# The last load of Wo in two pieces, and the residual's copies of x in four

## The chip, the cores and the metric

The kernel runs on one core of one Trainium2 chip. The metric is device time in microseconds of one execution, the median over several. A core has five engines with an instruction queue each: TensorE (PE; its weight loads are listed as PEld), VectorE (DVE), ScalarE (ACT), GpSimd (POOL) and SyncE (SP), and sixteen DMA engines that work on what the queues issue. In the profile SPq, ACTq and POOLq are the queues as issuers.

## What is computed

One decode step of an attention block beside a gated MLP, on 8 rows (batch 8, one token) of 512 numbers in bf16:

```python
xn = layernorm(x)
q  = xn @ wq                                # 32 heads of 128
k, v = the last 2048 of 8192 positions of the caches, 8 heads, each used by 4 query heads
s  = softmax(q k^T / sqrt(128)) v @ wo
g  = silu((sigmoid(xn @ w_gate) * (xn @ w_up)) @ w_down)
return x + s * g
```

The caches' windows are 64 MB, the weights another 13 MB; all are read once.

## The kernel before

**Tiles and loads.** Keys and values come in 32 tiles of 2 MB (`k_sb`, `v_sb`: one batch row and four of the eight heads each). They share a ring of ten buffers with the two halves of Wq, the three MLP weights and the two halves of Wo. All of these loads are issued on SP's queue, line 86, in one order: Wq's halves; key and value tiles, each value tile some slots behind its keys; the three MLP weights before the last two value tiles; last Wo. `issue_loads` issues as many as there are free buffers. The halves of Wo are cut: the first in two loads of 1 MB, the second in three of 512 KB and two of 256 KB (`load_wo`). The groups (h0, h1, j0, j1) of that list are the head groups and, in them, which of four interleaved rows j of Wo are loaded.

**The order of the work.** After the layer norm (`x_f` to `xnT_sb`, lines 259 to 287) PE makes q from `xnT_sb` and Wq. Then 64 slots follow: PE transposes a quarter of a key tile (line 395), DVE copies the result, PE multiplies by q (line 411); softmax runs once per batch row, and PE multiplies probabilities and values eleven slots later (line 513). After the last key slot comes the MLP, then the rest of the value products. The tail: 64 matmuls with Wo into `a_ps` (line 624; for each of eight head groups and four j, two column halves on different rows of PE's array), DVE's product with `gate` (`prod`, line 634), DVE's sum with x (`y_bf`, line 636), and two output transfers, on SP and ScalarE (line 638).

**The copies of x.** `x_bf` (line 92, ScalarE's queue) feeds the layer norm. The last sum uses another copy, `x2_sb` (`x_sb` in the profile, where digits are left out): columns 0 to 255 of x stand on partitions 0 to 7, columns 256 to 511 on partitions 32 to 39. GpSimd clears it (line 175) and issues its two loads (line 177), ahead of building the constants `ident`, `SumM` and `ones`, which DVE's constants and the layer norm's transposes need.

**Queues and counters.** Each queue runs its instructions in order; an instruction that waits holds up all behind it. The program's waits are made when it is built. Each transfer has a completion counter: those issued by SP and ScalarE share eight (0 to 7), given out in turn in the order of the built program, and GpSimd's have eight others. A transfer waits until the one that had its counter before has landed; so SP's loads have at most eight under way. `x_bf` has counter 0, Wq's halves 1 and 2, and the first key tile 3. At the end (line 667) SP waits for all counters and engines in a list of seven steps and a drain: counter 1; 2 and 0; 3 and GpSimd's second; 4 and GpSimd's first; 5 and DVE; 6 and PE; 7 and ScalarE; then GpSimd. A barrier over all engines follows.

Of the kernel before, what the change touches and what calls it, by code (L numbers as in the profile page):

```python
# [10 lines left out]
def kernel(  # L11
# [13 lines left out]
    nc = tc.nc  # L25
    P = 128
    B, _, D = A_x.shape
# [29 lines left out]
    DC = D // NCOL  # L57
# [25 lines left out]
    def load(dst, src, q=None):  # L83
        if q is None:
            q = nc.sync
        q.dma_start(out=dst, in_=src)

    def ring_tile(shape, name):
        return ring.tile(shape, bf16, name=name, tag="ring", align_bytes=ALIGN)
# [57 lines left out]
    def load_wo(half):  # L147
        t = ring_tile([P, HG // 2, 4, D], f"wo_sb{half}")
        for h0, h1, j0, j1 in (
            ((0, 2, 0, 4), (2, 4, 0, 4)),  # L150
            ((4, 5, 0, 4), (5, 6, 0, 4), (6, 7, 0, 4), (7, 8, 0, 2), (7, 8, 2, 4)),
        )[half]:
            o = half * (HG // 2)
            load(t[:, h0 - o : h1 - o, j0:j1, :], wo_view[:, h0:h1, j0:j1, :])
            for hg in range(h0, h1):
                for j in range(j0, j1):
                    wo_parts[hg, j] = t[:, hg - o, j, :]

    def issue_loads():
        while loads_done[0] < len(loads) and free_bufs[0] > 0:  # L160
            kind, i = loads[loads_done[0]]
            if kind == 0:
                k_tiles[i] = load_kv(A_k_cache, i, "k_sb")
            elif kind == 1:
                v_tiles[i] = load_kv(A_v_cache, i, "v_sb")
            elif kind == 2:
                load_mlp(i)
            else:
                load_wo(i)
            loads_done[0] += 1  # L170
            free_bufs[0] -= 1

    issue_loads()
    x2_sb = work.tile([NCOL * 32, DC], bf16, name="x2_sb")
    nc.gpsimd.memset(x2_sb[:], 0.0)
    for j in range(NCOL):
        nc.gpsimd.dma_start(
            out=x2_sb[32 * j : 32 * j + B, :],
            in_=A_x.flatten_outer_dims()[:, DC * j : DC * (j + 1)],
        )  # L180


    ident = consts.tile([P, P], bf16, name="ident")
# [3 lines left out]
    for off in range(-rep * (NJ - 1), rep * NJ, rep):  # L187
        nc.gpsimd.affine_select(
            out=SumM[:],
            in_=SumM[:],  # L190
# [9 lines left out]
        out=SumM_blk,  # L200
        in_=SumM_blk,
# [7 lines left out]
        out=SumM_blk,  # L209
        in_=SumM_blk,  # L210
# [11 lines left out]
        out=Jneg[:],  # L222
        in_=ident[:].rearrange("p (a j r) -> p j a r", j=NJ, r=rep),
# [4 lines left out]
        out=Jneg[:], in0=Jneg[:], scalar1=-scale, scalar2=None, op0=ALU.mult  # L228
# [4 lines left out]
        out=Hm[:],  # L233
        in_=ident[:].rearrange("p (a gl) -> p gl a", gl=GL),
# [6 lines left out]
        out=Sel[:],  # L241
        in_=ident[:].rearrange("p (a m) -> p m a", m=32),
# [6 lines left out]
        out=perm[:].rearrange("k (p gl) -> k p gl", gl=GL),  # L249
        in_=ident[:].rearrange("k (gl p) -> k p gl", gl=GL),  # L250
# [17 lines left out]
        out=rstd[:], in_=mv[:, 1:2], func=AF.Sqrt, bias=eps_t[:], scale=1.0  # L268
# [4 lines left out]
        out=xn_bf[:],  # L273
# [7 lines left out]
    for kt in range(KT):  # L281
        nc.tensor.transpose(  # L282
            out=xnT_ps[:, kt, :], in_=xn_bf[:B, kt::KT], identity=ident[:B, :B]
# [353 lines left out]
    for c in range(NCOL):  # L637
        queues[c].dma_start(
            out=out.flatten_outer_dims()[:, DC * c : DC * (c + 1)],
            in_=y_bf[32 * c : 32 * c + B, :],  # L640
# [31 lines left out]
```

## Time and profile before

| what | value |
|---|---|
| median of 3 runs | 199.86 us (199.71 to 199.94) |
| the profiled execution: its own time | 199.68 us |
| its span, first to last instruction | 197.9 us |
| PE busy, share of the span | 156.5 us, 79% |
| DVE busy | 121.7 us, 62% |
| ACT busy, POOL busy | 22.9 us, 7.4 us |
| moved by DMA | 81.33 MB, 6724 packets, mean 411 GB/s |
| loads of key tiles, issue to landing (median) | 38.9 us |
| loads of 256 KB of Wo: two, issue to landing (median) | 16.9 us |
| copies of x for the last sum: two of 4 KB, issue to landing (median) | 6.1 us |

Times in the profile are microseconds from the first instruction; durations of single instructions are in nanoseconds. A wait is put down to what ended it. The duration of a DMA instruction is that of its issue; a transfer is done at its landing. A median over an even number of transfers is the mean of the middle two: the two of 256 KB took 14.80 and 19.07 us.

### The profile page before, as it was taken

How to read it: one execution, taken by the hardware profiler on the slowest of the kernel's cores; microseconds unless marked ns; L12 is line 12 of the kernel's file. 1: busy time of each engine (PE TensorE's matmuls, PEld its weight loads, DVE VectorE, ACT ScalarE, POOL GpSimd, SP SyncE). 2: the span in 40 equal slices, each digit the busy share in tenths (PEclk: the TensorE clock that was granted, in tenths of full speed). 3: DMA queues.
4: the chain of work that ended last, by engine and by line, in shares of the span. 5: the costliest groups of instructions: out<-in, count | busy, mean ns of one | idle time of the engine just before them, and what ended most of it. 6: DMA issues, size and time to landing. Idle time of an engine off the chain costs nothing.

```text
span 197.9 us, 4704 instructions
## 1 busy us (share of the span) xinstructions
PE 156.5 (79%) x2088; PEld 102.2 (52%) x2088; DVE 121.7 (62%) x256; ACT 22.9 (12%) x48; POOL 7.4 (4%) x20
## 2 busy tenths in 40 slices
PE   0164999689979898968996979697999896757692
PEld 0113766456646555635564656464755573244581
DVE  2607788687787587748774677278758775231211
ACT  2001000500110021002100110012002102400000
POOL 7700000000000000000000000000000000000000
PEclk9999999999999999999998899979999999675558
DMA  6999999999999999999999999999999999999980
GB/s 227 429 427 440 437 421 427 421 439 424 431 427 427 427 434 427 431 427 431 427 431 432 421 434 427 437 421 431 427 424 440 426 424 432 428 425 420 416 331 31
DMA packets 6724, 81.33 MB, mean 411 GB/s; under 512 B 776, under 2 KB 816, under 8 KB 1968
## 3 DMA queue, kind: packets, MB, share of 16 engines
q1 hardware_dynamic: 6608, 81.01, 96.4%
q8 instruction: 16, 0.26, 0.5%
q10 hardware_dynamic: 32, 0.01, 0.1%
q14 instruction: 4, 0.03, 0.0%
q0 software_dynamic: 64, 0.01, 0.0%
HBM read 81.02 MB, written 0.01 MB: 409 GB/s over the span
## 4 chain that ended last, share of the span: by engine, by line
DMA 89%; PE 7%; DVE 2%; issue 0%; SPq 0%
DMA k_sb<-in_A_k_cache_dram 60%; DMA v_sb<-in_A_v_cache_dram 18%; DMA wo_sb<-in_A_wo_dram 7%; DMA wq_sb<-in_A_wq_dram 4%; PE kT_ps L395 4%; PE s_ps L411 1%; DVE kT_sb L398 1%; PE acc_ps L513 1%; DVE pT_sb L473 1%; DVE pt_bf L451 0%; DVE prod L634 0%; DVE y_bf L636 0%; PE a_ps L624 0%; PE pT_ps L457 0%; PE den_ps L495 0%
## 5 line engine op out<-in xcount | busy, mean ns | idle before, releaser
L398 DVE COPY kT_sb<-kT_ps 128x1024 bf16<-128x1024 bf16 x128 | 83.5, 687 | 35.6 <-PE kT_ps L395 35.0
L395 PE MATMUL kT_ps<-ident,k_sb 128*128 128x128 bf16 x1024 | 72.0, 226 | 9.7 <-DMA k_sb<-in_A_k_cache_dram 9.5
L395 PEld LDWEIGHTS <-k_sb 128*128 128x128 bf16 x1024 | 62.2, 102 | 30.9 <-issue 16.7
L411 PE MATMUL s_ps<-kT_sb,qz_sb 128*32 128x512 bf16 x256 | 39.9, 612 | 0.0
L513 PE MATMUL acc_ps<-v_sb,pT_sb 128*32 128x256 bf16 x512 | 27.3, 300 | 4.1 <-DVE pT_sb L473 2.6
L513 PEld LDWEIGHTS <-pT_sb 128*32 128x32 bf16 x512 | 13.0, 105 | 16.6 <-issue 12.0
L534 PEld LDWEIGHTS oT_ps<-Sel,acc_sb 128*128 128x128 f32 x64 | 9.6, 215 | 9.2 <-issue 5.8
L526 ACT COPY acc_sb<-acc_ps 128x256 f32<-128x256 f32 x16 | 5.9, 372 | 70.0 <-PE acc_ps L513 70.0
L534 PE MATMUL oT_ps<-Sel,acc_sb 128*128 128x16 f32 x64 | 11.1, 289 | 2.0 <-ACT acc_sb L526 1.1
L437 ACT ACTIVATE p_bf<-s_ps,nm 128x512 bf16<-128x512 f32 x8 | 5.5, 687 | 49.2 <-DVE nm L434 49.2
L411 PEld LDWEIGHTS <-qz_sb 128*32 128x32 bf16 x256 | 6.6, 93 | 6.9 <-issue 0.8
L457 PE MATMUL pT_ps<-pt_bf,perm 128*128 128x512 bf16 x8 | 3.1, 385 | 7.7 <-DVE pt_bf L451 7.7
L473 DVE TENSOR_SCALAR pT_sb<-pc_bf,Hm 128x512 bf16<-128x512 bf16 x32 | 9.0, 345 | 0.0
L282 PE MATMUL xnT_ps<-ident,xn_bf 8*128 8x8 bf16 x4 | 0.3, 174 | 8.7 <-DVE xn_bf L272 8.7
L451 DVE STREAM_TRANSPOSE pt_bf<-p_bf 128x512 bf16<-128x512 bf16 x8 | 5.6, 704 | 1.7 <-ACT p_bf L437 1.7
L541 DVE TENSOR_TENSOR oT_sb<-oT_ps,rden 128x16 bf16<-128x16 f32 x16 | 2.7, 171 | 6.0 <-PE oT_ps L534 6.0
L624 PE MATMUL a_ps<-wo_sb,o_sb 128*32 128x256 bf16 x64 | 6.2, 369 | 0.2 <-DMA wo_sb<-in_A_wo_dram 0.2
L423 DVE TENSOR_REDUCE mx<-s_ps 128x1 f32<-128x512 f32 x8 | 5.5, 682 | 0.6 <-PE s_ps L411 0.6
L348 PE MATMUL q_ps<-wq_sb,xnT_sb 128*32 128x512 bf16 x32 | 3.8, 627 | 2.2 <-DMA wq_sb<-in_A_wq_dram 2.0
L624 PEld LDWEIGHTS <-o_sb 128*32 128x32 bf16 x64 | 4.9, 131 | 1.2 <-issue 0.4
L465 ACT CAST pc_bf<-pT_ps 128x512 bf16<-128x512 f32 x8 | 4.7, 586 | 6.6 <-PE pT_ps L457 6.6
L497 DVE RECIPROCAL rden<-den_ps 128x32 f32<-128x32 f32 x8 | 2.9, 358 | 4.2 <-PE den_ps L495 4.2
(61 smaller groups left out, 56.1 us busy)
## 6 DMA issues: line engine op xcount, KB each, us to landing
k_sb<-in_A_k_cache_dram SPq DMA_DIRECT2D x16, 2048.0 KB, 38.9
v_sb<-in_A_v_cache_dram SPq DMA_DIRECT2D x16, 2048.0 KB, 39.3
wq_sb<-in_A_wq_dram SPq DMA_DIRECT2D x2, 2048.0 KB, 9.7
wo_sb<-in_A_wo_dram SPq DMA_DIRECT2D x2, 1024.0 KB, 32.3
wg_sb<-in_B_w_gate_dram SPq DMA_DIRECT2D x1, 1792.0 KB, 38.2
wu_sb<-in_B_w_up_dram SPq DMA_DIRECT2D x1, 1792.0 KB, 35.3
wd_sb<-in_B_w_down_dram SPq DMA_DIRECT2D x1, 1792.0 KB, 37.0
wo_sb<-in_A_wo_dram SPq DMA_DIRECT2D x3, 512.0 KB, 24.1
```

The source lines that it names most:

```text
L395: nc.tensor.transpose(out=kT_ps[:, jj, :], in_=k_sb[:, c0 + jj, :], identity=ident[:, :])
L398: nc.vector.tensor_copy(out=kT_tiles[t][:, h2 * HALF : (h2 + 1) * HALF, :], in_=kT_ps[:])
L411: nc.tensor.matmul(s_tiles[b][XR * gl : XR * (gl + 1), :], lhsT=qz_sb[:, b, GL * gg + gl, z0 : z0 + XR], rhs=kT[:, :, gl::GL], start=(x == 0),
L423: nc.vector.reduce_max(out=mx[:], in_=s_tiles[b][:], axis=AX.X)
L437: nc.scalar.activation(out=p_bf[:], in_=s_tiles.pop(b)[:], func=AF.Exp, bias=nm[:], scale=scale, accum_out=den128[:],)
L451: nc.vector.transpose(out=pt_bf[:], in_=p_bf[:])
L465: nc.scalar.copy(out=pc_bf[:], in_=pT_ps[:])
L473: nc.vector.tensor_scalar(out=pT_tiles[b][:, :, gl, :], in0=pc, scalar1=Hm[:, gl : gl + 1], scalar2=None, op0=ALU.mult,)
L513: nc.tensor.matmul(acc_tiles[i][32 * c : 32 * (c + 1), :], lhsT=pT_tiles[b][:, x * (CC // 2) + n, :, :].rearrange("p g n -> p (g n)"), rhs ...
L526: nc.scalar.copy(out=acc_sb[:], in_=acc_tiles.pop(i)[:])
L534: nc.tensor.matmul(oT_ps[:], lhsT=acc_sb[:, Dh * c2 : Dh * (c2 + 1)], rhs=Sel[:].rearrange("p (g c r) -> p c g r", g=GL, c=2)[:, c2], star ...
L624: nc.tensor.matmul(a_ps[32 * c : 32 * (c + 1), :], lhsT=o2_sb[:, hg, j, :], rhs=wo_parts[hg, j][:, DC * c : DC * (c + 1)], start=(n == 0), ...
```

## The change

The last 256 KB of Wo (head group 7, j = 2 and 3) are loaded as two transfers of 128 KB, one for each j, so that a partition's row of the transfer has 1 KB in place of 2. The two loads of `x2_sb` become four, each of four rows and 256 columns; the first column half is issued by GpSimd in two, the second by ScalarE in two. In the code they stand where the two stood: after the first round of loads and after GpSimd's clearing, ahead of the constants; on ScalarE that is behind `x_bf` and ahead of the layer norm's square root (line 267).

```diff
@@ load_wo
         for h0, h1, j0, j1 in (
             ((0, 2, 0, 4), (2, 4, 0, 4)),
-            ((4, 5, 0, 4), (5, 6, 0, 4), (6, 7, 0, 4), (7, 8, 0, 2), (7, 8, 2, 4)),
+            ((4, 5, 0, 4), (5, 6, 0, 4), (6, 7, 0, 4), (7, 8, 0, 2), (7, 8, 2, 3), (7, 8, 3, 4)),
         )[half]:
@@ after the first issue_loads()
     x2_sb = work.tile([NCOL * 32, DC], bf16, name="x2_sb")
     nc.gpsimd.memset(x2_sb[:], 0.0)
+    BH = B // 2
     for j in range(NCOL):
-        nc.gpsimd.dma_start(
-            out=x2_sb[32 * j : 32 * j + B, :],
-            in_=A_x.flatten_outer_dims()[:, DC * j : DC * (j + 1)],
-        )
+        for h in range(2):
+            (nc.gpsimd, nc.scalar)[j].dma_start(
+                out=x2_sb[32 * j + BH * h : 32 * j + BH * (h + 1), :],
+                in_=A_x.flatten_outer_dims()[
+                    BH * h : BH * (h + 1), DC * j : DC * (j + 1)
+                ],
+            )
```

## The prediction

> **What bounds the kernel now.** I read the page first, for the share of the transfers and the chain that ended last.
>
> ```profile
> span 197.9 us, 4704 instructions
> ...
> DMA  6999999999999999999999999999999999999980
> ...
> DMA 89%; PE 7%; DVE 2%; issue 0%; SPq 0%
> ```
>
> The reader is to see that the sixteen DMA engines are full from the second of forty slices to the last but two: 81 MB at 411 GB/s is the kernel. The change alters no bytes of any size, so what it can move lies before the stream starts or after its end. The chain of waits in order of time shows the end (start, duration, what):
>
> ```profile
> 179.27 14.80 DMA wo_sb<-in_A_wo_dram
> 194.07 0.04 issue
> 194.11 0.41 PE a_ps L624 x4
> 194.52 0.02 issue
> 194.55 0.42 DVE prod L634
> 194.97 0.02 issue
> 195.00 0.42 DVE y_bf L636
> ```
>
> The last piece of Wo is issued at 179.27, lands at 194.07, and only the four matmuls that read it (j = 2 and 3, two column halves each), the product and the sum follow. The windows of the tail (engine columns, then granted clock, DMA share, GB/s) say whether PE could use an earlier piece:
>
> ```profile
> 190.00:191.00 1.00, 1.00 (x14) 0.85 (x10) 0.00 (x0) 0.00 (x0) 0.00 (x0) 0.50 0.97 379
> 191.00:192.00 1.00, 1.00 (x14) 0.83 (x12) 0.00 (x0) 0.00 (x0) 0.00 (x0) 0.50 0.59 225
> 192.00:193.00 1.00, 1.00 (x16) 0.90 (x14) 0.00 (x0) 0.00 (x0) 0.00 (x0) 0.66 0.55 217
> 193.00:194.00 1.00, 0.92 (x16) 0.59 (x11) 0.00 (x0) 0.00 (x0) 0.00 (x0) 1.00 0.33 125
> ```
>
> PE is busy to 193.92, at half clock until about 192.7, and starves only for the last 0.19 us. The DMA share of 0.55 to 0.59 says that about half of the engines were done by 191 and the other half run on to 193.8.
>
> Then the start, from the timeline of all engines (the first number in brackets is idle time before, then its cause):
>
> ```profile
> 0.80 0.60 ACTq L92 DMA_DIRECT2D x_bf<-in_A_x_dram  x1
> 1.41 1.17 POOL L177 DMA_DIRECT2D x_sb<-in_A_x_dram  x2 [0.30 <-POOL x_sb L175]
> 1.44 1.28 ACT L267 ACT_TABLE_LOAD   x1 [1.44 <-PEq L656]
> 7.57 0.29 ACT L267 ACTIVATE rstd<-mv,eps_t 8x1 f32<-8x1 f32 x1 [4.85 <-DVE eps_t L265]
> 13.10 1.90 PE L348 MATMUL q_ps<-wq_sb,xnT_sb 128*32 128x512 bf16 x16 [1.97 <-DMA wq_sb<-in_A_wq_dram]
> ```
>
> ScalarE's queue is free from 2.72 (end of the table load) to 7.57, and PE waits 1.97 us for the second half of Wq, which is cover for anything that delays the layer norm. Last, SP's waits at the end (total, times, longest) and its semaphore instructions of the closing line:
>
> ```profile
> SPq L638 <- DMA wo_sb<-in_A_wo_dram: 5.1, 1, 5.1
> ...
> SPq L667 <- DMA out_dram<-y_bf: 0.2, 1, 0.2
> ```
>
> ```profile
> L667 SPq EVENT_SEMAPHORE  x9: 17/28/28, 195.9 to 197.8; - x9
> ```
>
> The first row is the rule of the eight completion counters: SP's output transfer may not start before the transfer that used its counter last has landed, here the first piece of Wo at 186.6. The 0.2 is in the closing list of waits: four of its seven steps had run before the outputs were in, and it stopped at the counters of the two output transfers (landed at 196.73 and 196.91).
>
> **The split piece.** It adds one issue on SP and one wait on PE, and takes two of four matmuls from behind the last landing. The matmuls go in pairs: the records of the last four start at 194.114, 194.117, 194.222 and 194.237. With half of the piece there earlier, one pair runs before the last landing, so the end comes one pair earlier: -0.11 us. The data itself: an engine carries eight rows of the piece, each record of 2 KB takes 84 ns, and the 1 KB rows of x_bf take 44, so sixteen of them cost 16 x 44 - 8 x 84 = 32 ns more, and the counter's 4-byte record 9: +0.04. The first half lands some 0.3 us before the second (the two pieces of 256 KB land 0.59 apart: 174.41 + 19.07 = 193.48 against 194.07), about 193.8, before PE is through at 193.92, so the pair finds it there. If it did not, the 0.11 is lost; if the last half came half a piece earlier too, the gain would be 0.4. I take 0.07, by these records. The added issue must wait for the landing eight transfers before, the last v tile, at 184.11. The seven issues of Wo took between 0.34 and 3.73 us, so it is out by 187.9 at the latest, and the engines come to it only after 190: hidden by over 2 us; without that cover it would cost the difference directly.
>
> The Trainium skill ("DMA: Bandwidth & Descriptors", "Anatomy of one DMA" and "Rules for kernel authors") speaks against this: each transfer has about 2.0 us of fixed cost, and halves for disjoint partitions are said not to be worth it, since both run on the same engines. If that fixed cost came after the first half, the kernel would stand near 201.9. The row above, two landings 0.59 apart, says that the fixed part of a queued transfer overlaps with the one before it, so I leave it out.
>
> **The copies of x.** GpSimd issues two before and two after, of half the rows. The rows are 652 and 521 ns. If an issue cost half with half the rows, ident would be built 0.6 us earlier; if it cost double, 1.2 later. Behind the issues on GpSimd stand ident and SumM, behind ident DVE's constants, the cast of x and the layer norm; Q's first matmul would move from 9.23 to between 8.6 and 10.4 and its 1.90 us would end by 12.3, under the second half of Wq at 13.07. Nothing either way; without the 1.97 us of cover it would be the shift itself. ScalarE gets two issues between x_bf and the table load. ScalarE's rows are 597 ns (x_bf) and 308 ns (output), so 0.6 to 1.2 us; the table load ends by 3.9 at the latest, and rstd waits for DVE until 7.57. Nothing, with 3.7 us of cover. The 8 KB are the same packets of 512 B (27 ns each on an engine). DVE's last sum has to wait on four transfers in place of two: one more semaphore instruction of 50 ns, which like the present one (194.56) runs under the product's 0.41 us.
>
> **The counters.** Two transfers that had GpSimd's counters now take two of the eight that SP and ScalarE share. Counters go out in the order of the built program, not of the text; there, GpSimd's copies of x already stand ahead of the second load of Wq, since that order counts a 2 MB load as long on its queue. ScalarE's two copies should stand there too and get counters never used before: no wait. SP then has five unused counters in place of seven, so its fifth to eighth tiles, issued at 4.84 to 13.07 now, come out at 8.4 to 13.1, when the landings of Wq release them; at 8.4 five loads of 2 MB at 4.9 us each are queued before them, so the stream has 24 us of cover. From the next load on every wait is for the same tile as now.
>
> At the end the count matters. Before the two output transfers there are 45 now (x_bf, two of Wq, 35 tiles, seven pieces of Wo), so they take counters 5 and 6 of 0 to 7. After, there are 48 = 6 x 8, and they take 0 and 1. The closing list on SP waits in a fixed order: 1; then 2 with 0; 3; 4; 5; 6; 7; then GpSimd. Now the outputs stop it at 5 and 6, and after counter 6 (196.926) one more step (196.991) and the drain (197.058) remain. After the change the first step of all waits for SP's output, and six steps follow: **five more of them exposed**. The steps after 196.926 are 0.065 and 0.067 apart, two earlier ones 0.059 and 0.089; five by 0.066 is +0.33. The ends: 5 x 0.017 (the busy time of such an instruction alone) = 0.09, and 5 x 0.089 plus one step of 0.477 that the list showed between 195.915 and 196.392, on counters that had long been done, with 0.089 taken off: 0.83. I take 0.33 because the same instructions after the same kind of wait showed it.
>
> **Sum.** -0.11 + 0.04 + 0.33 = +0.26 us on a profiled execution of 199.68 (span 197.9 and 1.8 around it): 199.94. The median of the runs is 199.86, 0.18 above that execution, so the forecast there is 200.12, 0.13% up. 0.2%, or 0.40 us, is about what a measurement of this kernel can tell from no change: 199.46 to 200.26.
>
> **Rivals.**
> - The closing list costs nothing more (other counters than I count, or its steps run ahead of the landing). For: four of seven do so now. Against: the counters go strictly in turn. Then -0.07 alone: 199.8.
> - The step of 0.477 comes after the outputs as well. For: nothing it waited for was open. Against: if SP was occupied with the output transfer's issue (195.44), that is over by 196.9. It decides if the span grows between the output's landing and GpSimd's final barrier by over 0.5: 0.26 + 0.41 = +0.67: 200.5, slower.
> - ScalarE's two copies come after ten loads of SP in the counters' order, as in the text. Then they wait for the first two k tiles (17.93 and 22.83), and the table load and rstd behind them on ScalarE: rstd from 7.57 to about 24.8, Q's matmuls from 9.23 to 26.4, the first transposes of k from 17.95 to 30.2. Of these 12.3 us PE wins back its later waits for k (9.5 in all less the first 2.96) and about 3.8 after 169 (2.26, 0.82 and 0.70): some 2.0 stay: 201.9. It decides as soon as rstd runs later than Q's cover of 1.97 us. Against it speaks the built order of GpSimd's copies.
> - The late half of the DMA engines gets less behind, because GpSimd's copies (64 small packets) shrink. PE's stalls of 0.35 and 0.11 before the last pieces could then go, 0.46 at most: 199.4 with a free list, 199.7 with mine. Little speaks for it: 16 KB against 81 MB.
>
> **How the numbers follow.** Forecast 0.51, of which 0.09 ends above 200.26; free list 0.14; the long step 0.17; ScalarE held up 0.08; earlier engines 0.10, to which 0.02 of the free list's lower end is added as faster. Slower 0.09 + 0.17 + 0.08 = 0.34, faster 0.12, within 0.2% the rest, 0.54. The range runs from 199.5 (half of the faster cases) to 200.9 (the long step at its dearest end, 199.86 - 0.07 + 0.83, with 0.3 for a last half that lands late); outside are ScalarE's case and half of the faster ones, some 0.15.
>
> **What would show it.** The last four matmuls in two separated pairs, the last landing within 0.1 us of 194.1; rstd still at 7.6; SP's closing steps all after the output's landing, seven of them in place of three, and the span 0.2 to 0.4 longer. Wrong would be: an ACT wait of over 5 us on a k tile, closing steps that still run before 196.5, or a last landing that moves by more than 0.3 us.

## The result and the profile after

| | before | after |
|---|---|---|
| median of the runs, measured side by side | 199.82 us (199.71 to 199.94) | 200.72 us (200.67 to 200.79) |
| ratio, with its 95% interval | | 1.0045 (1.0028 to 1.0062) |
| the profiled execution: its own time | 199.68 us | 200.69 us |
| its span | 197.9 us | 198.7 us |
| the rest, outside the span | 1.8 us | 2.0 us |

The change makes the kernel slower by 0.90 us, 0.45%. The forecast was 200.1, with 200.72 inside its range of 199.5 to 200.9; but the likeliest case was "within 0.2%", and what happened is what the second rival described, with 0.2 us on top that no case had.

The page of after, in the lines that were shown of before:

```profile
span 198.7 us, 4708 instructions
...
DMA  6999999999999999999999999999999999999970
...
DMA 91%; PE 6%; SPq 0%; DVE 0%; issue 0%
```

The stream is as full as before from the second slice on. The last digit but one is 7 in place of 8: the span has grown behind the stream, not in it. The chain of waits in order of time (start, duration, what) shows the end:

```profile
184.22 10.02 DMA wo_sb<-in_A_wo_dram
194.24 0.04 issue
194.28 0.30 PE a_ps L628 x2
194.59 0.02 issue
194.61 0.42 DVE prod L638
195.03 0.02 issue
195.06 0.42 DVE y_bf L640
```

Two matmuls in place of four lie behind the last landing, and PE's part falls from 0.41 to 0.30: the pair of the split piece is gained as forecast. The landing itself is at 194.24 in place of 194.07, so that `y_bf` starts at 195.06 in place of 195.00. These two cancel, all but 0.06. The windows of the tail (length, busy time of PE, PEld, DVE, ACT and POOL, granted clock, DMA share, GB/s) agree:

```profile
192.00:193.00 1.00, 0.76 (x14) 0.56 (x11) 0.00 (x0) 0.00 (x0) 0.00 (x0) 1.00 0.56 217
193.00:194.00 1.00, 0.97 (x14) 0.67 (x14) 0.00 (x0) 0.00 (x0) 0.00 (x0) 1.00 0.41 143
```

PE is busy nearly to 194 (0.97 us of the last row, 0.92 before). The start, from the timeline of all engines:

```profile
1.41 1.16 POOL L179 DMA_DIRECT2D x_sb<-in_A_x_dram  x2 [0.30 <-POOL x_sb L175]
1.45 0.60 ACTq L179 DMA_DIRECT2D x_sb<-in_A_x_dram  x2
2.08 1.28 ACT L271 ACT_TABLE_LOAD   x1 [2.08 <-POOL x_sb L175]
7.55 0.29 ACT L271 ACTIVATE rstd<-mv,eps_t 8x1 f32<-8x1 f32 x1 [4.19 <-DVE eps_t L269]
13.04 1.90 PE L352 MATMUL q_ps<-wq_sb,xnT_sb 128*32 128x512 bf16 x16 [1.93 <-DMA wq_sb<-in_A_wq_dram]
```

GpSimd's two issues take 1.16 us, as they did with twice the rows; ScalarE's two take 0.60 and push the table load from 1.44 to 2.08; `rstd` stays at 7.55 and Q's second half at 13.04. Nothing is lost here. What is left is the end. First SP's waits there (total, times, longest), then the instructions of the closing line on SP from the output's landing to the drain (duration in ns as least, median, greatest; first and last start):

```profile
SPq L671 <- DMA out_dram<-y_bf: 1.1, 1, 1.1
```

```profile
L671 SPq EVENT_SEMAPHORE  x7: 17/28/28, 197.0 to 197.8; - x7
L671 SPq DRAIN  x1: 13/13/13, 197.9 to 197.9; - x1
```

The closing list now waits 1.1 us for an output where it waited 0.2, and all seven of its instructions start after the landing. In the trace's records the two lists read so (starts in us):

| | landing of SP's output | the steps of the list | drain | landing to drain |
|---|---|---|---|---|
| before | 196.91 | 195.856, 195.915, **gap of 0.477**, 196.392, 196.481, 196.746, 196.926, 196.991 | 197.058 | 0.15 |
| after | 196.95 | 196.970, **gap of 0.466**, 197.436, 197.525, 197.595, 197.667, 197.731, 197.793 | 197.858 | 0.91 |

From the drain to the end of the span it is 0.83 us in both. So the span's 0.80 is 0.04 up to the output's landing and 0.76 in the closing list, and of that 0.76 more than half is the one long step, which used to run while the outputs were under way. The other 0.2 of the profiled execution lies outside the span.

### The profile page after: what moved, and what is told of

It reads as the page before. It is cut to its first block, busy times and chain, and to the rows that moved or that the text cites. A ratio compares the mean times of both kernels' runs of the same rounds, so it can differ in the third digit from the quotient of the medians.

```text
span 198.7 us, 4708 instructions
## 1 busy us (share of the span) xinstructions
PE 153.8 (77%) x2088; PEld 101.2 (51%) x2088; DVE 121.2 (61%) x256; ACT 22.9 (12%) x48; POOL 7.4 (4%) x20
## 4 chain that ended last, share of the span: by engine, by line
DMA 91%; PE 6%; SPq 0%; DVE 0%; issue 0%
DMA k_sb<-in_A_k_cache_dram 67%; DMA v_sb<-in_A_v_cache_dram 19%; DMA wo_sb<-in_A_wo_dram 5%; PE kT_ps L399 4%; PE s_ps L415 1%; SPq L86 0%; DVE prod L638 0%; DVE y_bf L640 0%; PE a_ps L628 0%
## 5 line engine op out<-in xcount | busy, mean ns | idle before, releaser
L517 PE MATMUL acc_ps<-v_sb,pT_sb 128*32 128x256 bf16 x512 | 26.2, 290 | 4.2 <-DVE pT_sb L477 2.6
L517 PEld LDWEIGHTS <-pT_sb 128*32 128x32 bf16 x512 | 12.5, 103 | 16.6 <-issue 12.3
L367 DVE STREAM_TRANSPOSE qT_sb<-q_sb 128x512 bf16<-128x512 bf16 x2 | 1.4, 712 | 6.0 <-ACT q_sb L365 6.0
```

Of the source, the lines that this page charges most:

```text
L517: nc.tensor.matmul(acc_tiles[i][32 * c : 32 * (c + 1), :], lhsT=pT_tiles[b][:, x * (CC // 2) + n, :, :].rearrange("p g n -> p (g n)"), rhs ...
```

## The experiments

The change has two independent parts, and there were three accounts of the loss: the closing list, longer because the outputs take other counters (my theory, then with the long step in it); the copies of x or the split piece themselves; and, once the 0.2 outside the span was seen, some cost behind the last instruction.

**Part by part.** The split alone:

```diff
-            ... (7, 8, 0, 2), (7, 8, 2, 4)),
+            ... (7, 8, 0, 2), (7, 8, 2, 3), (7, 8, 3, 4)),
```

> Only the last piece of Wo is split; the copies of x stay as before. 46 transfers stand before the outputs, so these take counters 6 and 7. Theory list (the end of the kernel is longer because SP's closing list has more steps behind the output's landing): the list stops at its last step and only the drain follows, 0.065 us less than before; the last landing and the earlier pair of matmuls give +0.06 as in the changed kernel: 199.8, between 199.6 and 199.95. Theory split (the halves of 1 KB rows and the extra transfer cost the time): 200.6 to 200.8. Theory copies (the four copies of x cost it): 199.75 to 199.9.

Measured: 199.65 us beside 199.83, ratio 0.9989 (0.9980 to 0.9998). This kernel is a little faster than before and after; part of that can be its place in the closing list, told below. Its chain of waits, and its closing line from 196.9 on:

```profile
184.25 10.01 DMA wo_sb<-in_A_wo_dram
194.26 0.04 issue
```

```profile
L667 SPq EVENT_SEMAPHORE  x1: 28/28/28, 197.0 to 197.0; - x1
L667 SPq DRAIN  x1: 13/13/13, 197.1 to 197.1; - x1
```

One transfer more before the outputs gives them counters 6 and 7, the last places of the list: one step and the drain are left behind the landing, not two and the drain as before.

The copies of x alone, as the change has them, with Wo as before:

```diff
-        nc.gpsimd.dma_start(... 8 rows ...)
+        for h in range(2):
+            (nc.gpsimd, nc.scalar)[j].dma_start(... 4 rows ...)
```

> Only the copies of x are changed, in halves over GpSimd's and ScalarE's queues; the last piece of Wo is whole. 47 transfers stand before the outputs: ScalarE's takes counter 7, SP's counter 0, which is in the second step of the closing list. Theory list: the step of 0.477 us and five short ones of about 0.07 come after the landing in place of one: +0.69, so 200.5, between 200.35 and 200.65. Theory split: 199.75 to 199.9. Theory copies: 200.6 to 200.8; theory list and theory copies are told apart by the next two kernels.

Measured: 200.63 us, ratio 1.0036 (1.0024 to 1.0049). Two transfers more give the outputs counters 7 and 0. The list can do its first step, and then stands in the second; its semaphore instructions from 196.0 on:

```profile
L671 SPq EVENT_SEMAPHORE  x6: 28/28/1011, 196.0 to 197.8; - x6
```

The 1011 ns are the wait for SP's output, which landed at 197.01; it ends at 197.04. The next step starts at 197.49, 0.45 later: that is the long step. Four more steps and the drain follow. So the loss comes with the copies, but this run doesn't say whether by their place or by their number.

The whole change, but with all four copies on GpSimd, whose counters are others, so that the outputs take 6 and 7:

```diff
-            (nc.gpsimd, nc.scalar)[j].dma_start(
+            nc.gpsimd.dma_start(
```

> Both parts of the change, but all four copies of x are issued by GpSimd, so they take none of the eight counters that SP and ScalarE share: 46 before the outputs, which take 6 and 7. Theory list: 199.8, between 199.6 and 199.95, with the split and the halves both in. Theory split: 200.6 to 200.8. Theory copies, if halves as such cost: 200.6 or more, since GpSimd now issues four; if only ScalarE's queue costs: 199.8.

Measured: 199.88 us beside 199.83, ratio 1.0000 (0.9991 to 1.0008). The same pieces cost nothing that can be told from before when they don't take the shared counters. Beside split_only they cost 0.23 us, most of it outside the span (1.95 in place of 1.79 us, in the table below).

**The counters without the change.** The kernel before, with three loads of four rows of x into a tile that nothing reads, on ScalarE's queue behind the copies:

```diff
+    idle = work.tile([3 * 32, DC], bf16, name="idle")
+    for m in range(3):
+        nc.scalar.dma_start(
+            out=idle[32 * m : 32 * m + 4, :],
+            in_=A_x.flatten_outer_dims()[0:4, 0:DC],
+        )
```

> The kernel before with three more loads on ScalarE's queue (four rows of 256 columns each, into a tile that nobody reads), where ScalarE issues its copies in the changed kernel. Neither Wo nor the copies of x are touched. 48 transfers before the outputs, as in the changed kernel: counters 0 and 1. Theory list: SP stops at the first step, and the step of 0.477 and five more follow: +0.76, so 200.6, between 200.4 and 200.75. Theory split: 199.85. Theory copies: 199.85, unless loads on ScalarE's queue as such cost; then in proportion to their number, 200.7 to 201.2.

Measured: 200.59 us beside 199.83, ratio 1.0039 (1.0026 to 1.0051). SP's wait at the end and its closing line:

```profile
SPq L673 <- DMA out_dram<-y_bf: 1.1, 1, 1.1
```

```profile
L673 SPq EVENT_SEMAPHORE  x7: 17/28/28, 197.1 to 197.9; - x7
L673 SPq DRAIN  x1: 7/7/7, 198.0 to 198.0; - x1
```

The same two pictures as in the kernel after, with neither the split nor the halves: 0.76 us by the medians, and nothing was added but transfers whose data nobody uses. With one and two such loads the count can be walked through:

> The kernel before with one idle load of four rows on ScalarE's queue at the start. 46 transfers before the outputs: counters 6 and 7, the last step of the list. Theory list: 0.065 less than before or equal, 199.8, between 199.6 and 199.95. Theory that a load on ScalarE's queue costs as such: a third of what three of them cost, +0.25, 200.1.

> The kernel before with two idle loads on ScalarE's queue at the start. 47 transfers before the outputs: counters 7 and 0; the list stops at its second step. Theory list: as with only the copies changed, 200.5 to 200.7, so a jump of 0.7 to 0.9 over one idle load. Theory cost for each load: two thirds of three, 200.35.

Measured: 199.72 us, ratio 0.9996 (0.9987 to 1.0005), with one; 200.48 us, ratio 1.0035 (1.0022 to 1.0048), with two; before stood at 199.78 in both. The second load, not the first, costs 0.76. The waits at the end, of the kernel with one and of the kernel with two:

```profile
SPq L673 <- DMA out_dram<-y_bf: 0.2, 1, 0.2
```

```profile
SPq L673 <- DMA out_dram<-y_bf: 1.0, 1, 1.0
```

A cost per load would have shown with the first. It is a matter of places: counters 6 and 7 are waited for last, 0 in the second step.

**The list behind the change.** The kernel after, with eight loads of 64 bytes on SP between the last load of Wo and the outputs. In the built program SP's output still has counter 1, so the list stops at its first step as in the kernel after; ScalarE's output, which that order puts among the loads, has 6:

```diff
+    idle = work.tile([8, 32], bf16, name="idle")
+    for m in range(8):
+        nc.sync.dma_start(
+            out=idle[m : m + 1, :], in_=A_x.flatten_outer_dims()[0:1, 0:32]
+        )
     a_ps = ...
```

> The changed kernel with eight more loads of 64 bytes on SP's queue, into a tile nobody reads, between the last load of Wo and the outputs. Eight take each counter round once, so SP's output still has counter 1 and the closing list still stops at its first step; but SP's closing instructions stand eight places later in its program. Theory place (the step of about 0.47 us comes at one place of SP's instruction stream, the 82nd instruction, wherever the list stands): that place now lies among the added loads, where SP waits anyway, and the list runs in short steps after the landing: 0.47 less than the changed kernel, 200.25, between 200.1 and 200.4. Theory closing (the long step belongs to the list or to the output transfer): 200.7, between 200.6 and 200.9.

Measured: 199.94 us beside 199.78, ratio 1.0005 (0.9996 to 1.0014): below the range that either theory gave, though "place" had the direction. Its closing line:

```profile
L676 SPq EVENT_SEMAPHORE  x7: 17/28/28, 196.8 to 197.1; - x7
L676 SPq DRAIN  x1: 13/13/13, 197.2 to 197.2; - x1
```

All seven stand behind the landing of SP's output, as in the kernel after, but they run from 196.756 to 197.128 with the drain at 197.193: 0.44 us, and no long step among them. This is the run that parts the two sizes. Six steps to the drain's start and no long one take 0.44, against 0.13 for one step and the drain before: 0.31 more, where the forecast had 0.33. The long step has gone with its place: in every kernel here whose list holds the 82nd instruction of SP's part of the built program (the 80th of SP's records in the trace), the step stands before that one, wherever in the list it falls; in copies_only and two_idle it comes just after the wait for an output. In eight_late that instruction is among the added loads, where SP waits anyway. There is a second difference: SP's output landed at 196.74, before ScalarE's at 196.94, where elsewhere it landed second; the list passes its first step 0.2 earlier for it, which is most of what the expectation missed.

**The long step alone.** I tried to put the long step behind the landing with the outputs still on counters 5 and 6, by taking four instructions from SP ahead of the list: three loads go to ScalarE's queue, the first half of Wo becomes one load of 2 MB, and one idle load restores the count.

```diff
-        load(t[:], wq_view[...])
+        load(t[:], wq_view[...], (nc.sync, nc.scalar)[kh])
@@ load_kv: the first two loads
+            nc.scalar if loads_done[0] < 2 else nc.sync,
@@ load_wo
-            ((0, 2, 0, 4), (2, 4, 0, 4)),
+            ((0, 4, 0, 4),),
@@ behind the copies of x
+    nc.scalar.dma_start(out=idle[0:4, :], in_=A_x.flatten_outer_dims()[0:4, 0:DC])
```

> The kernel before with four transfers fewer on SP's queue: the second half of Wq and the first two key tiles go out on ScalarE's queue, and the first half of Wo is one load of 2 MB in place of two. One idle load on ScalarE's queue keeps the count at 45, so the outputs have counters 5 and 6 as before, and Wo's last pieces are as before. Only the place of SP's closing list in its program is changed: its last step is now the 82nd instruction, behind the output's landing. Theory place: the span grows by the long step less a short one, 0.47 - 0.065 = 0.40, and the closing records show the long step between the sixth and the seventh: 200.25, between 200.05 and 200.5 with what the new start order may add or take. Theory closing (the long step belongs to the list's beginning, some 0.5 us after the output's issue): it stays before the landing, 199.85, between 199.65 and 200.0.

Measured: 200.90 us beside 199.84, ratio 1.0048 (1.0034 to 1.0061), outside what was expected. The closing line and PE's timeline:

```profile
L670 SPq EVENT_SEMAPHORE  x2: 28/28/28, 198.3 to 198.8; - x2
L670 SPq DRAIN  x1: 34/34/34, 198.9 to 198.9; - x1
```

```profile
189.35 6.54 PE L627 MATMUL a_ps<-wo_sb,o_sb 128*32 128x256 bf16 x64 [0.75 <-DMA wo_sb<-in_A_wo_dram]
```

The place came out: two steps behind the landing, as before, but 0.477 apart (198.303 and 198.780), and landing to drain is 0.58 in place of 0.15. The total can't be used: with the first half of Wo in one transfer, Wo's matmuls start at 189.35 in place of 188.13, and the product (195.94 in place of 194.55) comes 1.39 us later, which has nothing to do with the list. In the records the list itself takes 0.43 more from landing to drain, where 0.40 was expected. As a test of the size by the total it failed; as a test of where the step goes it holds.

**Outside the span.** In the records, the kernels whose DVE has 317 instructions in the built program (315 in the trace, against 314) show one more 8 KB fetch of instructions after the span (in the kernel after at 200.48); those with 316 show none there. The change brings DVE from 316 to 317: four copies of x are waited for by two semaphore instructions, not one. So: the kernel before with one instruction more on DVE, and the kernel after with one less.

```diff
@@ before, behind the clear of eps_t
+    idle = small.tile([B, 1], f32, name="idle")
+    nc.vector.memset(idle[:], 0.0)
@@ after
-    nc.vector.memset(eps_t[:], 1e-5)
+    nc.gpsimd.memset(eps_t[:], 1e-5)
```

> The kernel before with one more instruction on DVE, a clear of 8 numbers beside the one of eps_t at 7.5 us; DVE has 317 instructions in place of 316, as in the changed kernel, and nothing else changes (counters 5 and 6, Wo and the copies of x as before). Theory tail (the fourth copy of x gives DVE a second semaphore instruction, and with it the program's 317th brings one more fetch of 8 KB of instructions after the span, 0.2 us): span 197.9 as before, the profiled execution 2.0 longer than its span in place of 1.8, the median 200.0, between 199.9 and 200.15. Theory noise (the four kernels with 2.0 around the span had it by chance or from the copies as such): 199.8.

> The changed kernel with the clear of eps_t on GpSimd in place of DVE; DVE has 316 instructions again. rstd then waits for GpSimd, whose clears end near 9.0, some 1.5 us later than now, under Q's cover of 1.93. Theory tail: span 198.7 as in the changed kernel, 1.8 around it, the median 200.5, between 200.35 and 200.65. Theory noise: 200.7.

Measured: 199.93 us beside 199.88 with one more, ratio 1.0004 (0.9995 to 1.0012); 200.52 us with one less, ratio 1.0031 (1.0019 to 1.0044), where after had 1.0045. By the medians alone the first isn't told from no change. The time outside the span is the sharper measure; mean over all runs of a kernel, with the least and greatest (each is a run's time less its span, which is given to 0.1):

| kernel | DVE instructions | runs | outside the span, us |
|---|---|---|---|
| before, beside all experiments | 316 | 67 | 1.80 (1.75 to 1.87) |
| split_only | 316 | 11 | 1.79 (1.75 to 1.85) |
| three_idle | 316 | 5 | 1.79 (1.76 to 1.80) |
| one_idle | 316 | 11 | 1.81 (1.76 to 1.85) |
| two_idle | 316 | 5 | 1.79 (1.76 to 1.81) |
| long_step_alone | 316 | 5 | 1.83 (1.80 to 1.85) |
| one_less_dve | 316 | 6 | 1.80 (1.76 to 1.84) |
| after | 317 | 4 | 1.98 (1.87 to 2.05) |
| halves_on_gpsimd | 317 | 11 | 1.95 (1.79 to 2.07) |
| eight_late | 317 | 11 | 1.95 (1.82 to 2.04) |
| copies_only | 317 | 5 | 1.92 (1.83 to 2.05) |
| one_more_dve | 317 | 11 | 1.92 (1.72 to 2.05) |

One instruction more on DVE, a semaphore instruction or a clear, adds 0.11 to 0.17 us to the 1.80 in the mean, not in every execution; taking one away gives it back.

## Why the prediction was partly right and partly wrong

**The split piece: right in its mechanism.** The pair is gained (PE's part behind the last landing falls from 0.41 to 0.30 in the chain: 0.11, as forecast), though the first half landed at 193.91, not 193.8. In the profiles the last landing is at 194.23 to 194.29 in the five kernels with the split and the usual order, and at 194.07 to 194.31 in those without, on average about 0.07 later with it, where I had 0.04: the records of 1 KB took 46 ns in place of 44, so that 16 x 46 - 8 x 84 + 9 = 73 ns. Before's 194.07 is the earliest of all, so most of the 0.17 between the two profiles shown is spread between executions. The medians say somewhat more gain: split_only is at -0.18, and one_idle, which shares only its place in the list, at -0.06, so the split itself is worth about 0.12 by the medians and 0.04 by these rows of the traces; the intervals of the two medians together leave some 0.25 either way, so that a gain from the split alone is not shown. The Trainium skill ("DMA: Bandwidth & Descriptors", "Anatomy of one DMA") gives about 2 us of fixed cost for a transfer on GpSimd's path; here, on SP's queue, the two pieces land 0.33 us apart, at 193.91 and 194.24, so no such cost is paid again by the one that is queued behind the other. Its rule against two transfers ("Rules for kernel authors") is for disjoint halves of the partitions; the two pieces of Wo fill the same 128 partitions, so the prediction brought it up where it does not bear, and no run here tests it. The added issue on SP waited for the v tile that landed at 184.21 and was out at 184.55; the range of 184 to 188 held, and the cover of 2 us was not needed.

**The copies of x: right for what I costed, but a term is missing.** GpSimd's two issues take 1.16 us in place of 1.17, ScalarE's 0.60 (forecast 0.6 to 1.2), and the cover holds. DVE's additional semaphore instruction runs under the product, as written; I costed it at nothing on that ground, and one DVE instruction more is what brings the time outside the span from 1.80 to 1.98. A cost there wasn't in the trace of before to be read, and no end of the range was kept for it.

**The counters: right.** No wait of ScalarE for a k tile (that rival fell: `rstd` at 7.55), SP's early tiles out later without any gap in the stream, the outputs on counters 0 and 1, all seven steps after the landing, five of them newly exposed.

**The price of the list: wrong, and this is the step that failed.** "I take 0.33 because the same instructions after the same kind of wait showed it." Five short steps would have cost that, and where the long step is elsewhere they do (0.31 in eight_late). But one of the five was the long step: 0.47 for it, 0.29 for the other four, 0.76 in all. The row with 0.477 was in the prediction, with 0.83 as the dear end, and I put it to the cheap side because it stood soon after the issue of SP's output, which might have held SP up; that nothing it waited for was open spoke for the dear one. The runs show that it doesn't follow the issue: it stays before the same instruction of SP, wherever in the list that falls. In the kernel before it was hidden only since the list ran ahead while the outputs were in flight. The question that I should have asked is the one I put for other edits: what hides this row now, and is the cover still there? A list that is stopped at its first step loses all of its cover, and with it the long step's. That the time is inside the range is partly luck: the dear end of the list allowed for the long step, but it took the 0.3 kept for a late landing to cover the time outside the span, which no case had.

**The sum.** With the sizes as the runs have them: -0.12 to -0.04 for the split, +0.76 for the list (three_idle, by its median), +0.17 outside the span, +0.81 to +0.89 together, beside 0.90 (0.56 to 1.24) measured. What is left is within the interval. Earlier DMA engines, the last rival, did not show: the DMA share of the last windows before 194 is 0.56 and 0.41, against 0.55 and 0.33, no less work left at the end than before.

**What stays open.** What causes the long step is not shown; its place in SP's instructions is. The records hold a hint: in every kernel of which a trace was kept, an 8 KB fetch of instructions starts 1.06 to 1.35 us after the end of SP's instruction before the step (in before at 197.02, that instruction having ended at 195.94; in after at 198.09 and 196.99). It does so in eight_late too, at 191.81 and 190.71, where the step itself is hidden in a wait. So the long step may be the time that SP spends on having more instructions fetched; no run here separates the two. That the 0.2 outside the span is the extra fetch itself is likely from the records, but shown is only that one instruction on DVE switches both.

## What to carry to other kernels

A small transfer isn't paid for only where it runs: each takes a completion counter from a shared ring, and the count of transfers before the outputs decides where the closing list of waits stops; read that list in the trace, with all of its steps, and let the outputs take the counters that it waits for last. Here the split alone (199.65 us), or the whole change with GpSimd's counters for the copies (199.88 us), keeps the list short, and the first is the version to use. Where a wait moves ahead in a list, every step behind it loses its cover, the dear one too: price each with its own row, not with the mean of its neighbours.

## What the runs showed of the hardware

- SP takes 0.45 to 0.48 us before one certain instruction, the 82nd of its part of the program, with nothing open that it waits for (0.466 in after, 0.477 in before, 0.467 in three_idle). Among loads that SP waits for, as in eight_late, it cost nothing; at the end it is a quarter of a percent.
- DVE with 317 instructions in place of 316 lengthens the time outside the span by 0.11 to 0.17 us in the mean, and an 8 KB fetch of instructions appears there.
- Two output transfers of the same size, issued at about the same time by SP and ScalarE, land some 0.2 us apart (196.73 and 196.91 before), and which of them is first can change: with eight small loads ahead of it on SP's queue, SP's came first.
